# Attention of the first eight pairs in four 64x64 tiles of the array, two pairs at a time, with another order of the early work

## The chip, the core and the metric

The kernel runs on one core of a Trainium2 chip. The metric is the device time of one launch in microseconds, as the median of several runs. Before the change it is 834.56 us (three runs, 834.26 to 834.79). PE is the matrix engine, PEld its loading of stationary operands; DVE, ACT and POOL are the vector, scalar and general engines; SP issues nearly all DMAs.

## The reference

Attention over blocks of 64 positions, for 8 batches of 576 positions and 8 heads of 64, and then a feed-forward layer with g = h - tanh(h):

```python
q_c = q.reshape(B, H, nc, chunk, D)            # chunk = D = 64; k_c, v_c alike
scores = scale * np.matmul(q_c, k_c.transpose(0, 1, 2, 4, 3))
scores = scores - np.max(scores, axis=-1, keepdims=True)
attn = np.exp(scores)
attn = attn / (np.sum(attn, axis=-1, keepdims=True) + 1e-09)
out = np.matmul(attn, v_c)
...
x = np.ascontiguousarray(attn_out.transpose(0, 2, 1, 3)).reshape(B * S, H * D)   # 4608 x 512
h = x @ w_in          # 512 x 2048
g = h - np.tanh(h)
return (g @ w_out).astype(np.float32)
```

The weights arrive as 64-bit floats, 16.8 MB, and are made into 32-bit ones in the kernel.

## The kernel before, in words

The 4608 tokens are 36 **pairs**: 128 tokens, two blocks of 64 positions, all 8 heads. Four pairs are a **group** of the feed-forward layer, nine groups in all. Groups 2 to 8 have another attention (class `Late`, f16) and another feed-forward; the change leaves them alone. It is about the **early pairs** 0 to 7, the tokens of groups 0 and 1, and about the order of the work up to the end of group 0.

An early pair p goes through these steps (class `Early`; the letter is its token in the plan):

- `a`, `v`: DMAs of q and k, and of v. q and v lie in tiles `qbd`, `vbd` twice as wide, whose other half is zero, so that the product of a 128-row operand gives two blocks at a time on the whole array. The zeros are written once, at the start, by DVE and ACT (L172, L174).
- `S`: scores, 8 f32 products of 128x128 by 128x64 into a PSUM bank (L195).
- `M` or `E`: the maximum of each row (DVE, L202), then either subtraction on DVE and one exponent on ACT (`M`), or eight exponents on ACT that also sum (`E`, L213).
- `N` or `n`: sums, reciprocals and division of the weights, on DVE (`N`, L228) or by head on ACT (`n`, L226).
- `T`: four transposes on PE (L156), copied from PSUM by ACT (`aT`).
- `V`: values, 8 products (L243), and the result as a rounded part `xh` (ACT, L250) and a rest `xl` (DVE, L251).

The weights of the feed-forward come in 16 units `fc`. `l` loads a half of a unit (part 0 of w_in, part 1 of w_out; three buffers), `c` converts: one ACT and three DVE instructions put the bits together (L141 to L144), then ACT rounds to `wh` and DVE takes the rest `wl` (L148, L149). `g` is gemm1 of a unit (12 products `xh wh`, `xh wl`, `xl wh`, L552) with h - tanh(h) behind it (ACT L563, DVE L564) and a split into `gh` and `gl` (ACT L571, DVE L572). `h` is gemm2 of the oldest unit that is split (12 products, L581). With a part behind the dot, `l`, `c` and `g` do a half; half a gemm1 covers two pairs. `F` is a number of idle products on a tile of zeros, which nothing reads (L819).

The text `PLAN` (L55) is the order of these tokens. Left of the bar, SP and PE run in just the order written, while the order on the other engines follows a scheduler; right of it the place in the text is a rank, and a scheduler lays out all engines. `Y` ends the first pair of PSUM banks, after which scores, transposes and values have one pool of two banks; `Z` frees the attention's tiles for the later weights. In every case each engine's order is fixed when the program is built, and an instruction that waits holds up all behind it on its engine.

## Time and profile before

| | before |
|---|---|
| median of 3 runs | 834.56 us |
| the profiled execution's own time | 834.37 us |
| its span | 832.5 us |
| PE busy | 819.0 us, 98% of the span |
| DVE, ACT, POOL busy | 650.1, 474.6, 375.0 us |
| DMA | 63.17 MB, 234 GB/s in the first fortieth of the span |
| first gemm1 of group 0 | 27.70 us |
| last gemm2 of group 0 | ends about 142.4 us |

A busy PE is not a PE at its peak: the ends of products are modelled and overlap, so a row's duration is longer than the distance to the next. In a row of the timeline, the first number is the start, the second the length in us, then engine, line, operation, what is written and read, shape and count. A group of instructions by line shows busy time in us, then the mean of one in ns, then the engine's idle time before them.

### The profile page before, as it was taken

What the parts mean: (1) busy time and instruction counts of PE and PEld (TensorE: products, weight loads), DVE (VectorE), ACT (ScalarE), POOL (GpSimd) and SP (SyncE); (2) the same over time, 40 slices, a digit from 0 to 9 for tenths busy, and PEclk for the clock granted to TensorE, in tenths of its full rate; (3) what the DMA queues carried; (4) which work ended last, traced back from release to release, by engine and by line L of the source; (5) the groups of instructions that cost most, each with busy time, mean ns of one, the idle gap of its engine ahead of it and who ended that gap; (6) DMA issues with size and microseconds to landing.
All of it is one profiled execution on the core that took longest, in us unless ns stands there. A gap on an engine that the chain in (4) does not pass through costs nothing.

```text
span 832.5 us, 20121 instructions
## 1 busy us (share of the span) xinstructions
PE 819.0 (98%) x8546; PEld 686.5 (82%) x8546; DVE 650.1 (78%) x879; ACT 474.6 (57%) x779; POOL 375.0 (45%) x380
## 2 busy tenths in 40 slices
PE   8999999999999999999999999999999999999997
PEld 6888777778866657878888888888888888888886
DVE  5897797785755998899787878787878787877553
ACT  6798785865453546674565456545654564454332
POOL 0000000000015874857575757575757575757563
PEclk9999999999999999999999999999999999999999
DMA  9865245131110212322222322222222220302000
GB/s 234 238 223 165 103 153 172 55 102 53 27 52 1 78 26 78 77 78 52 78 52 77 53 78 51 78 51 78 52 78 51 78 52 3 52 2 51 2 27 26
DMA packets 64858, 63.17 MB, mean 76 GB/s; under 512 B 33024, under 2 KB 47360, under 8 KB 64768
## 3 DMA queue, kind: packets, MB, share of 16 engines
q1 hardware_dynamic: 64480, 61.62, 26.5%
q8 instruction: 67, 1.10, 0.6%
q10 hardware_dynamic: 288, 0.26, 0.1%
q14 instruction: 23, 0.19, 0.1%
HBM read 45.09 MB, written 9.44 MB: 65 GB/s over the span
## 4 chain that ended last, share of the span: by engine, by line
PE 85%; DVE 8%; POOL 2%; issue 2%; ACT 1%; DMA 1%; SPq 0%; DVEq 0%; ACTq 0%
PE ph L649 28%; PE po L689 25%; PE po L581 13%; PE ph L552 12%; PE psa L343 3%; PE psa L195 2%; PE psa L243 1%; DVE gl L572 1%; DVE w L143 1%; DMA vbd<-vE 1%; DVE w L144 1%; DVE wh L515 1%; DMA k<-kE 0%; DVE wl L515 0%; DVE wl L149 0%
## 5 line engine op out<-in xcount | busy, mean ns | idle before, releaser
L649 PE MATMUL ph<-xh,wl 128*128 128x256 f16 x2160 | 249.6, 273 | 0.0
L649 PEld LDWEIGHTS <-wl 128*128 128x128 f16 x2160 | 209.9, 98 | 25.1 <-issue 0.5
L658 POOL TENSOR_TENSOR xl<-xl 128x256 f32<-128x256 f32 x96 | 96.9, 1009 | 184.1 <-DVE xl L657 183.4
L656 ACT ACTIVATE t<-ph,sig 128x512 f32<-128x512 f32 x96 | 65.8, 685 | 147.8 <-PE ph L649 147.1
L689 PEld LDWEIGHTS <-wh 128*128 128x128 f16 x1008 | 98.6, 98 | 11.4
L657 DVE SCALAR_TENSOR_TENSOR xl<-ph,sig,t 128x512 f32<-128x512 f32 x96 | 71.6, 746 | 46.6 <-ACT t L656 46.4
L659 POOL TENSOR_TENSOR xl<-xl 128x128 f32<-128x128 f32 x96 | 105.4, 1098 | 0.0
L660 POOL TENSOR_TENSOR xl<-xl 128x256 f32<-128x256 f32 x96 | 92.9, 968 | 0.0
L689 PE MATMUL po<-wl,wh 128*128 128x256 f16 x576 | 89.7, 273 | 0.0
L670 DVE SCALAR_TENSOR_TENSOR wh<-xl,to_g,wh 128x896 f16<-128x896 f32 x48 | 64.6, 1346 | 30.0 <-ACT wh L669 30.0
L669 ACT ACTIVATE wh<-xl,to_g 128x896 f16<-128x896 f32 x48 | 49.9, 1039 | 60.7 <-POOL xl L660 60.7
L581 PE MATMUL po<-wh,gh 128*128 128x512 f32 x192 | 79.1, 412 | 0.7 <-ACT gh L571 0.7
L670 DVE SCALAR_TENSOR_TENSOR gl<-xl,to_g,gh 128x896 f16<-128x896 f32 x48 | 71.9, 1498 | 8.9 <-ACT gh L669 8.7
L552 PE MATMUL ph<-xh,wl 128*128 128x512 f16 (+2 forms) x324 | 77.1, 375 | 0.0
L581 PE MATMUL po<-wh,gl 128*128 128x512 f32 x192 | 75.3, 397 | 1.0 <-DVE gl L572 1.0
L689 PE MATMUL po<-wh,wh 128*128 128x256 f16 x432 | 75.9, 273 | 0.0
L581 PE MATMUL po<-wl,gh 128*128 128x512 f32 x192 | 75.5, 393 | 0.0
L689 PEld LDWEIGHTS <-gh 128*128 128x128 f16 x672 | 64.9, 98 | 7.8
L458 POOL PARTITION_ALL_REDUCE whole<-sums x1 | 0.4, 445 | 131.9 <-DMA rawv<-vL 131.9
L689 PE MATMUL po<-wh,gh 128*128 128x256 f16 x336 | 54.4, 273 | 0.0
L572 DVE TENSOR_TENSOR gl<-t,gh 128x512 fp32r<-128x512 f32 (+1 forms) x52 | 40.2, 776 | 17.9 <-ACT gh L571 15.6
L689 PE MATMUL po<-wl,gh 128*128 128x256 f16 x336 | 52.4, 273 | 0.0
(158 smaller groups left out, 1502.6 us busy)
## 6 DMA issues: line engine op xcount, KB each, us to landing
raw<-w_in SPq DMA_DIRECT2D x16, 512.0 KB, 3.8
raw<-w_out SPq DMA_DIRECT2D x16, 512.0 KB, 5.6
rawk<-kL SPq DMA_DIRECT2D x28, 256.0 KB, 3.5
rawv<-vL SPq DMA_DIRECT2D x28, 256.0 KB, 3.5
xl<-qL SPq DMA_DIRECT2D x28, 256.0 KB, 2.9
out<-wh SPq DMA_DIRECT2D x46, 128.0 KB, 1.8
qbd<-qE SPq DMA_DIRECT2D x16, 128.0 KB, 4.2
k<-kE SPq DMA_DIRECT2D x8, 256.0 KB, 4.8
```

The costliest lines, as they stand in the source:

```text
L552: nc.tensor.matmul(ph, lhsT=self.weight(fc, 0, a)[:, kc * P:(kc + 1) * P], rhs=x[b][:, kc, cols], start=(k == 0), stop=(k == 3 * KC - 1))
L572: nc.vector.tensor_sub(gl, t, gh)
L581: nc.tensor.matmul(self.po[t], lhsT=gg[a][:, ts], rhs=self.weight(fc, 1, b), start=(fc == 0 and i == 0), stop=(fc == FC - 1 and i == 2))
L649: nc.tensor.matmul(self.ph[:, 1 - f::2, :], lhsT=half_w[fc][:, w, kc * P:(kc + 1) * P], rhs=rhs, start=(k == 0), stop=(k == 3 * KC - 1))
L656: nc.scalar.activation(t, self.ph, AF.Tanh, scale=sig)
L657: nc.vector.scalar_tensor_tensor(out=u[:, :4], in0=self.ph, scalar=sig, in1=t, op0=ALU.mult, op1=ALU.subtract)
L658: nc.gpsimd.tensor_add(u[:, 4:6], u[:, 1:3], u[:, 0:4:3])
L659: nc.gpsimd.tensor_add(u[:, 6], u[:, 1], u[:, 2])
L660: nc.gpsimd.tensor_sub(u[:, 0:4:3], u[:, 0:2], u[:, 2:4])
L669: nc.scalar.activation(gh, u, AF.Copy, scale=powers[1])
L670: nc.vector.scalar_tensor_tensor(out=gl, in0=u, scalar=powers[1], in1=gh, op0=ALU.mult, op1=ALU.subtract)
L689: nc.tensor.matmul(place[m], lhsT=part[:, self.SUM[m]], rhs=w[m][:, o], start=first, stop=(last and part is gl), skip_group_check=True)
```

## The change

q, k and v of the early pairs are laid out anew, and `p` in the tokens `a`, `S`, `v` now stands for one block (of 64 positions) of both pairs of a couple: rows 0 to 63 of its tile belong to the first pair, rows 64 to 127 to the second. There are no zeros. Each product has a 64x64 stationary operand in one of the four quarters of the array; a method `products` gives them out, quarter after quarter. Two PSUM banks take a couple's scores, one bank per pair, and each bank is filled half by the first `S` and half by the second. The values of both pairs are computed at the second of them, and their result is written by two copies and two subtractions for two pairs. The DMAs write 2 KB per row in one piece where they wrote 512 bytes at a time. The plan is a new text. It has 21 idle products where there were 29, six `E` and two `M` where there were five and three, two `n` and six `N` where there were three and five.

```diff
 PLAN = """
-a0 a1 l0.0 l0.1 a2 v2 F4 F1 v0 F4 S0 v1 l1.0 S1 l1.1 F1 c0 F1 a3 F6 l2.0 c1 F1 E0 N0 T0 S2 F4 l3.0 M1 M2 n1 T1 N2 V0 V1 F7 v3 S3 T2 g0.0 M3 V2 l2.1 N3 T3 V3 | g1.0 c2 l3.1 a4 l4.0 l4.1 v4 g0.1 h c3.0 Y S4 l5.0 g2.0 a6 g3.0 E4 c3.1 h n4 a5 l5.1 c4.1 h l6.0 c4.0 l7.0 g2.1 h g3.1 v6 l6.1 h l7.1 c5 S5 E5 g1.1 g4 S6 E6 h N5 c7.0 n6 g7 c6.0 l8.0 v5 a7 v7 T4 h T5 l8.1 V5 c7.1 c6.1 g6 T6 V4 l9.0 h V6 S7 E7 N7 T7 V7 Z l10.0 h c8 l11.0 h l11.1 l10.1 l9.1 g5 c9 g8 g9 c10.0 h c10.1 l12.0 c11 h l13.0 l12.1 c12 g10 l14.0 h h c13.0 g11 l14.1 l15.0 h g12 l13.1 l15.1 c13.1 g13 h h c14.0 c14.1 c15 h g14 g15 h h
+l0.0 a0 a1 l0.1 F9 S0 S1 v0 v1 E0 M1 c0.0 l1.0 l1.1 a2 F8 N0 T0 a3 N1 T1 c0.1 F4 V0 c1.0 v2 v3 S2 S3 g0.0 l2.0 c1.1 E2 M3 g1.0 h l2.1 N2 T2 N3 T3 h V2 l3.0 | c2 l3.1 Y g0.1 g1.1 h a4 a5 l4.0 l4.1 S4 S5 v4 v5 c3 E4 E5 g2 h l5.0 l5.1 n4 N5 c4 g3 h T4 T5 V4 a6 a7 l6.0 l6.1 c5 g4 h S6 S7 v6 v7 c6 E6 E7 l7.0 l7.1 g5 h n6 N7 c7 T6 T7 V6 Z g6 h l8.0 l8.1 c8 g7 h l9.0 l9.1 c9 g8 h l10.0 l10.1 c10 g9 h l11.0 l11.1 c11 g10 h l12.0 l12.1 c12 g11 h l13.0 l13.1 c13 g12 h l14.0 l14.1 c14 g13 h l15.0 l15.1 c15 g14 h g15 h h
 """
...
-        def __init__(self, pool, psum, bufs, zeros):
+        def __init__(self, pool, psum, bufs):
...
-            self.qbd, self.vbd = (
-                [pool.tile([P, 4, P, 2], F32, name=f"{n}{i}", bufs=1) for i in range(bufs)] for n in ("qbd", "vbd")
-            )
...
+        def bank(self, p):
+            return self.psum[p // 2 % len(self.psum)].tile([P, 2, 4, CH], F32, name="psa")
 
         def load(self, p):
...
-            for c in range(2):
-                r = slice(c * CH, (c + 1) * CH)
-                nc.sync.dma_start(out=d["q"][r, :, r], in_=qE[p, c])
-            nc.sync.dma_start(out=d["k"], in_=kE[p])
+            for n, src in (("q", qE), ("k", kE)):
+                t = self.st[p][n] = self.pool.tile([P, H, CH], F32, name=n, bufs=self.bufs)
+                nc.sync.dma_start(out=t, in_=src[p])
...
+        def products(self, out, stationary, moving):
+            for hp in range(4):
+                for i, u in ((0, 0), (1, 1), (0, 1), (1, 0)):
+                    r = slice(i * CH, (i + 1) * CH)
+                    nc.tensor.matmul(out(i, hp)[u * D:(u + 1) * D], lhsT=stationary(r, hp, u), rhs=moving(r, hp, u), start=True, stop=True)
 
         def scores(self, p):
...
-            for h in range(H):
-                nc.tensor.matmul(ps[:, h, :], lhsT=d["q"][:, h // 2, :, h % 2], rhs=d["k"][:, h, :], start=True, stop=True)
+            if p == first:
+                for c in range(2):
+                    self.st[first + c]["sp"] = self.bank(p)
+            ps = [self.st[first + c]["sp"] for c in range(2)]
+            self.products(lambda c, hp: ps[c][:, p - first, hp], lambda r, hp, u: d["q"][r, 2 * hp + u], lambda r, hp, u: d["k"][r, 2 * hp + u])
...
         def values(self, p):
...
-            for hp in range(4):
-                for c in range(2):
-                    cs = slice(c * CH, (c + 1) * CH)
-                    nc.tensor.matmul(ps[:, hp, cs], lhsT=d["v"][:, hp, :, c], rhs=d["aT"][:, hp, cs], start=True, stop=True)
+            first = p // 2 * 2
+            ps = self.st[first]["vps"] = [self.bank(p) for _ in range(2)]
+            for c in range(2):
+                d = self.st[first + c]
+                self.products(lambda e, hp: ps[e][:, c, hp], lambda r, hp, u: d["v"][r, 2 * hp + u], lambda r, hp, u: d["aT"][r, hp, u * CH:(u + 1) * CH])
 
         def result(self, p, x, i):
...
-            nc.scalar.copy(out=xh[:, :, ts], in_=ps)
-            nc.vector.tensor_sub(xl[:, :, ts], ps, xh[:, :, ts])
+            for e, ps in enumerate(self.st.pop(p)["vps"]):
+                xh, xl = (t[:, :, ts].rearrange("p hp (c e q) -> p e c hp q", c=2, e=2)[:, e] for t in x)
+                nc.scalar.copy(out=xh, in_=ps)
+                nc.vector.tensor_sub(xl, ps, xh)
```

Line numbers behind `Early` are 7 lower in the changed kernel (L545 is L552 of before, L574 is L581).

How the order moves is shown at three places. The first is PE, from the values of the first pairs to the first gemm1. `psa<-aT,...` are values, `psa<-k,...` scores, `psa<-ident,s` transposes. Before (seven idle products stand ahead of these rows, and the values of pairs 0 and 1 ahead of those):

```order
L195 MATMUL psa<-k_218,qbd_132 128x64 x8
L156 MATMUL psa<-ident,s 128x128 x4
L552 MATMUL ph<-xh,wh_70 128x256 x4
L552 MATMUL ph<-xh,wl_71 128x256 x4
L552 MATMUL ph<-xl,wh_70 128x256 x4
L243 MATMUL psa<-aT,vbd_135 128x64 x8
```

Now:

```order
L177 MATMUL psa<-aT,v 64x64 x32
L177 MATMUL psa<-k,q 64x64 x32
L545 MATMUL ph<-xh,wh_70 128x256 x4
L545 MATMUL ph<-xh,wl_71 128x256 x4
L545 MATMUL ph<-xl,wh_70 128x256 x4
L545 MATMUL ph<-xh,wh_74 128x256 x4
```

Scores and values of two pairs stand together, and both come ahead of the first gemm1; the transposes of pairs 2 and 3 come after two half gemm1 and half a gemm2, all eight of them at once.

The second place is DVE at the same time, from the results of the first pairs on (`xl`), with the maxima `mx` of pairs 2 and 3. Before:

```order
L251 TENSOR_TENSOR xl<-psa,xh 128x4x128
L220 RECIPROCAL sm<-sm 128x8
L228 TENSOR_TENSOR s<-s,sm 128x512
L142 TENSOR_SCALAR w<-w 128x1024
L143 SCALAR_TENSOR_TENSOR w<-raw,w 128x1024
L144 SCALAR_TENSOR_TENSOR w<-raw,w 128x1024
L202 TENSOR_REDUCE mx<-psa 128x8
L208 TENSOR_TENSOR s<-psa,mx 128x512
```

Now:

```order
L244 TENSOR_TENSOR xl<-psa,xh 128x2x4x64 x2
L192 TENSOR_REDUCE mx<-psa 128x8 x2
L201 TENSOR_SCALAR mx<-mx 128x8
L142 TENSOR_SCALAR w<-w 128x1024
L198 TENSOR_TENSOR s<-psa,mx 128x2x4x64
L557 TENSOR_TENSOR t<-ph,t 128x256
L143 SCALAR_TENSOR_TENSOR w<-raw,w 128x1024
L565 TENSOR_TENSOR gl<-t,gh 128x256
```

Both maxima now stand behind the results of the first two pairs; before, pair 2 was already being divided there.

The third place is PE behind the scores of pairs 4 and 5: two gemm1 with half a gemm2 between them, and the transposes of these pairs. Before, the scores of one pair, other work, and the scores of the next:

```order
L195 MATMUL psa<-k_588,qbd_130 128x64 x8
L552 MATMUL ph<-xh,wh_74 128x256 x4
L552 MATMUL ph<-xh,wl_75 128x256 x4
L552 MATMUL ph<-xl,wh_74 128x256 x4
L552 MATMUL ph<-xh,wh_86 128x512 x4
L552 MATMUL ph<-xh,wl_87 128x512 x4
L552 MATMUL ph<-xl,wh_86 128x512 x4
L195 MATMUL psa<-k_529,qbd_131 128x64 x8
```

Now, from the second of the two gemm1 on:

```order
L545 MATMUL ph<-xh,wh_82 128x512 x4
L545 MATMUL ph<-xh,wl_83 128x512 x4
L545 MATMUL ph<-xl,wh_82 128x512 x4
L226 MATMUL psa<-ident,s 128x128 x6
L545 MATMUL ph<-xh,wh_86 128x512
```

The transposes of both pairs, six of eight at first, stand right behind that gemm1.

More of the change, by code (lines that the diff above doesn't have):

```diff
@@ new lines, in bank @@
+        def bank(self, p):
+            return self.psum[p // 2 % len(self.psum)].tile([P, 2, 4, CH], F32, name="psa")
+        def load(self, p):
+            for n, src in (("q", qE), ("k", kE)):
+                t = self.st[p][n] = self.pool.tile([P, H, CH], F32, name=n, bufs=self.bufs)
+                nc.sync.dma_start(out=t, in_=src[p])
+        def load_values(self, p):
+            v = self.st[p]["v"] = self.pool.tile([P, H, D], F32, name="v", bufs=self.bufs)
+            nc.sync.dma_start(out=v, in_=vE[p])
@@ L197, in largest @@
         def largest(self, p):
             d = self.st[p]
-            d["s"] = self.pool.tile([P, H, CH], F32, name="s", bufs=2)
-            d["mx"] = self.pool.tile([P, H, 1], F32, name="mx", bufs=2)
-            d["sm"] = self.pool.tile([P, H, 1], F32, name="sm", bufs=2)
-            nc.vector.reduce_max(out=d["mx"][:, :, 0], in_=d["sp"], axis=AX.X)
+            d["s"] = self.pool.tile([P, 4, 2, CH], F32, name="s", bufs=3)
+            d["mx"] = self.pool.tile([P, 2, 4, 1], F32, name="mx", bufs=3)
@@ L204, in exponents @@
+            d["sm"] = self.pool.tile([P, 4, 2, 1], F32, name="sm", bufs=3)
+            nc.vector.reduce_max(out=d["mx"].rearrange("p e hp k -> p (e hp k)"), in_=d["sp"].rearrange("p e hp k -> p (e hp) k"), axis=AX.X)
         def exponents(self, p, summed):
@@ L211, in exponents @@
             nc.vector.tensor_scalar_mul(d["mx"], d["mx"], -scale)
-            for h in range(H):
-                nc.scalar.activation(d["s"][:, h, :], d["sp"][:, h, :], AF.Exp, bias=d["mx"][:, h, :], scale=scale, accum_out=d["sm"][:, h, :])
+            for e in range(2):
+                for hp in range(4):
+                    nc.scalar.activation(d["s"][:, hp, e, :], d["sp"][:, e, hp, :], AF.Exp, bias=d["mx"][:, e, hp, :], scale=scale, accum_out=d["sm"][:, hp, e, :])
         def sums(self, p):
@@ L230, in transpose @@
         def transpose(self, p):
-            self.st[p]["aps"] = transposed(self.pool, self.psum[p % len(self.psum)], self.st[p]["s"])
+            d = self.st[p]
+            d["aps"] = self.bank(p).rearrange("p a b k -> p (a b k)").rearrange("p (hp n) -> p hp n", hp=4)
+            for hp in range(4):
+                nc.tensor.transpose(d["aps"][:, hp, :], d["s"][:, hp].rearrange("p e k -> p (e k)"), ident)
         def weights(self, p):
-            aT = self.st[p]["aT"] = self.pool.tile([P, 4, P], F32, name="aT", bufs=min(self.bufs, 2))
+            aT = self.st[p]["aT"] = self.pool.tile([P, 4, P], F32, name="aT", bufs=3)
@@ L235, in weights @@
             nc.scalar.copy(out=aT, in_=self.st[p]["aps"])
         def values(self, p):
-            d = self.st[p]
-            ps = d["vps"] = self.psum[p % len(self.psum)].tile([P, 4, P], F32, name="psa")
-            for hp in range(4):
-                for c in range(2):
-                    cs = slice(c * CH, (c + 1) * CH)
-                    nc.tensor.matmul(ps[:, hp, cs], lhsT=d["v"][:, hp, :, c], rhs=d["aT"][:, hp, cs], start=True, stop=True)
-        def result(self, p, x, i):
-            xh, xl = x
-            d = self.st.pop(p)
-            ps = d["vps"]
-            ts = slice(i * P, (i + 1) * P)
-            nc.scalar.copy(out=xh[:, :, ts], in_=ps)
-            nc.vector.tensor_sub(xl[:, :, ts], ps, xh[:, :, ts])
+            first = p // 2 * 2
@@ L799, in attn_ffn_kernel @@
     make_identity(nc, ident)
-    att = Early(pool, [psum, ps_a], 4, warm)
+    att = Early(pool, [psum, ps_a], 4)
     idle = ps_h.tile([P, MOST], F32, name="ph")
```

45 lines of the change are left out of this document (16 added, 29 removed).

## The prediction

> **What bounds the kernel now.** I read the page's busy shares first, then the time windows of the stage that the change touches, then the chain of waits inside it. The page and the windows (columns: stretch, its length, busy time and instruction count of PE, PEld, DVE, ACT, POOL, then the granted clock, DMA share, GB/s):
>
> ```profile
> PE 819.0 (98%) x8546; PEld 686.5 (82%) x8546; DVE 650.1 (78%) x879; ACT 474.6 (57%) x779; POOL 375.0 (45%) x380
> ...
> 16.50:27.70 11.20, 11.20 (x89) 9.96 (x88) 9.92 (x17) 8.09 (x21) 0.00 (x0) 1.00 1.07 299
> 27.70:39.00 11.30, 10.54 (x75) 9.13 (x74) 10.84 (x19) 7.86 (x18) 0.00 (x0) 1.00 0.73 194
> 39.00:60.00 21.00, 20.94 (x148) 19.23 (x147) 19.14 (x39) 19.14 (x64) 0.00 (x0) 1.00 0.68 219
> 60.00:80.00 20.00, 20.00 (x119) 17.16 (x119) 15.35 (x31) 17.60 (x59) 0.00 (x0) 1.00 0.50 156
> 80.00:100.00 20.00, 18.90 (x98) 15.33 (x98) 14.43 (x24) 13.99 (x39) 0.00 (x0) 1.00 0.42 154
> 100.00:142.40 42.40, 42.08 (x182) 33.19 (x181) 37.65 (x71) 32.98 (x71) 0.82 (x2) 1.00 0.41 134
> ```
>
> PE is the bound and has almost no holes after 16.5 us. Group 0 of the feed-forward ends at 142.4 us. Behind it PE's instructions are row for row the same in both kernels, so what group 0's end moves, the whole time moves. But DVE is no idle bystander: 10.84 of 11.30 us between 27.7 and 39.0, where the first softmaxes and the first weights compete for it. Less PE work helps only where DVE keeps up.
>
> **What the products cost.** From the chain of waits (start, us, what), then the timeline of PE asked up to 52.56, 52.67 and 52.78 us, and up to 171.10, 171.126 and 171.15 us:
>
> ```profile
> 39.17 0.88 PE psa L195 x8
> ...
> 58.74 1.82 PE psa L195 x16
> 60.56 2.85 PE po L581 x12
> 63.42 0.44 PE psa L156 x4
> ```
>
> ```profile
> 52.49 0.34 PE L195 MATMUL psa<-k,qbd 128*128 128x64 f32 x2
> 52.49 0.45 PE L195 MATMUL psa<-k,qbd 128*128 128x64 f32 x3
> 52.49 0.57 PE L195 MATMUL psa<-k,qbd 128*128 128x64 f32 x4
> ...
> 171.07 0.22 PE L343 MATMUL psa<-a,wh 64*64 64x64 f16 x4
> 171.07 0.25 PE L343 MATMUL psa<-a,wh 64*64 64x64 f16 x5
> 171.07 0.26 PE L343 MATMUL psa<-a,wh 64*64 64x64 f16 x8
> ```
>
> One pair's scores are 8 instructions and 16 records: an f32 product runs as two records on the same place of the array. 16 records take 1.82 us, 0.114 each. The first two start within 0.07 us of each other, the next 0.11 later each: the 64 columns stream in under 0.07, and the 128-column weights set the pitch. Values (L243) cost the same. So 8 pairs cost 16 x 1.82 = 29 us.
>
> In 64x64 tiles the weights have half the columns, so I estimate the pitch of one tile at half of 0.114, 0.06 us. How many tiles run together is the first unknown. The f16 rows show four records within 0.03 us, but the fifth, which needs the first tile again, starts only after 171.10, and 6 to 8 come behind it: a record whose tile is busy holds up all behind it. In f32 the second record of each product is such a record. So one product overlaps with the first record of the next alone, and costs one pitch: 32 products of two pairs take 32 x 0.06 = 1.9 us instead of 3.64. From below: four tiles always full, 64/4 x 0.06 = 0.96. From above: no overlap, 64 x 0.06 = 3.8. I take 1.9, because the f16 rows show the blocking itself. Each change between tiles and whole array I estimate at 0.1 us (the gap ahead of the first f16 tile record, 171.07, behind a product that began 0.33 before and streams 2.85/12 = 0.24), 0.2 per group.
>
> **The start.** From the timeline:
>
> ```profile
> 6.32 7.06 PE L195 MATMUL psa<-k,qbd 128*128 128x64 f32 x32 [1.12 <-DMA k<-kE]
> 13.17 3.72 PE L819 MATMUL ph<-warm 128*128 128x512 bf16 x9
> 17.16 2.00 PE L195 MATMUL psa<-k,qbd 128*128 128x64 f32 x16
> 18.99 1.03 PE L819 MATMUL ph<-warm 128*128 128x512 bf16 x4
> 20.29 3.88 PE L243 MATMUL psa<-aT,vbd 128*128 128x64 f32 x32
> ```
>
> The idle products (L819) take 0.41 us each at 13.17 and 0.26 at 18.99; scores take 0.22 a record at 6.32 and 0.12 at 17.16. PE runs at half clock until the end of the nine idle products. 7 us of scores alone did not lift it. How quickly the clock goes again, the end of the kernel shows (timeline of PE, then windows):
>
> ```profile
> 826.30 0.49 PE L689 MATMUL po<-wl,wh 128*128 128x256 f16 x3
> ...
> 826.80:828.80 2.00, 0.00 (x0) 0.00 (x0) 1.79 (x5) 0.17 (x1) 1.72 (x3) 1.00 0.01 3
> 828.80:830.80 2.00, 0.00 (x0) 0.00 (x0) 0.00 (x0) 0.00 (x0) 0.00 (x0) 0.50 0.78 262
> ```
>
> It fell to half 2 us after the last product. Now the changed start. SP loads one weight (0.52 MB) and four attention tiles (1.05 MB) before the first scores; from 2.1 us on, at 361 to 233 GB/s, that lands at 6.5 to 9 us. I take 8.5:
>
> ```profile
> 0.00:20.00 20.00, 17.71 (x76) 12.28 (x77) 11.43 (x23) 12.98 (x37) 0.69 (x6) 1.00 0.92 233
> 8.00:10.00 2.00, 2.00 (x12) 2.00 (x11) 0.00 (x0) 0.00 (x0) 0.00 (x0) 1.00 1.03 361
> ```
>
> Scores of pair 1 at half clock take 16 x 0.12 = 1.9, end 10.4 (before: 13.4). No softmax can begin sooner, since each bank now needs both halves. Then F8 keeps PE busy to 13.8. DVE's new order until s of pair 1 is divided counts 17 instructions. Their durations by form, and two single rows of the timeline:
>
> ```profile
> L149 DVE TENSOR_TENSOR wl<-w,wh 128x512 fp32r<-128x512 f32 x32 | 21.1, 686 | 2.2 <-ACT wh L148 2.1
> L144 DVE SCALAR_TENSOR_TENSOR w<-raw,w 128x1024 uint32<-128x1024 uint32 x9 | 10.9, 1215 | 0.1
> L143 DVE SCALAR_TENSOR_TENSOR w<-raw,w 128x1024 uint32<-128x1024 uint32 x9 | 10.9, 1221 | 0.1
> L142 DVE TENSOR_SCALAR w<-w 128x1024 uint32<-128x1024 uint32 x9 | 6.2, 687 | 0.0
> L142 DVE TENSOR_SCALAR w<-w 128x512 uint32<-128x512 uint32 x14 | 5.6, 417 | 0.3 <-ACT w L141 0.2
> L202 DVE TENSOR_REDUCE mx<-psa 128x8 f32<-128x512 f32 x8 | 5.5, 689 | 8.6 <-PE psa L195 8.6
> L220 DVE RECIPROCAL sm<-sm 128x8 f32<-128x8 f32 x8 | 1.6, 195 | 0.1
> ...
> 23.98 0.68 DVE L251 TENSOR_TENSOR xl<-psa,xh 128x512 fp32r<-128x512 f32 x1
> ...
> 34.40 0.69 DVE L228 TENSOR_TENSOR s<-s,sm 128x512 f32<-128x512 f32 x1
> ```
>
> Ten of 0.69 (128x512 forms, halves of L143 and L144 among them), two of 0.42, five of 0.17 to 0.2: 8.65 us. Such sums come out 6% long, since ends overlap: before, the 20 rows from 23.98 to 35.09 sum to 11.8 and took 11.1. So 8.1, and pair 1 is divided at 18.5. Between 13.8 and then PE has nothing but four transposes, 5 us, more than the 2 us in which the clock fell. So F4 (1.7), the values of pairs 0 and 1 (32 x 0.12 = 3.8) and the scores of 2 and 3 (3.8) run at half clock: 18.5 + 0.9 (transposes) + 1.7 + 3.8 + 3.8 = 28.7. From there DVE has the rows from the two maxima to the division of pair 3: 20 instructions, 11.3 us, less 6% is 10.6, plus 0.8 for the late first gemm1: 40.1. The last transposes (0.45), h of unit 1 (6 x 0.24 = 1.4) and the values of 2 and 3 (1.9) end at 43.9. Before, this same state, values of pair 3 done and the next scores about to start, is reached at 39.1 (row 39.17). **Late by 4.8 us.** What would hide it is the product work ready at that time, but PE's fixed order puts the transposes of 2 and 3 ahead of it. The new layout takes away DVE's and ACT's zeroing of the first 6 us; that time was not waited for past the first scores.
>
> **The rest of group 0.** Before: 142.4 - 39.1 = 103.3 us, of which about 99.5 is work (16 units of 24 products at 0.23 less the 5.6 done is 83, 8 x 1.82 of scores and values, 4 x 0.44 of transposes), 3.8 waiting. Now the work is less by 8 x 1.82 - 4 x 1.9 = 7.0, plus 6 x 0.2 of switching: 93.7. Waiting grows. First, behind the division of pair 3 DVE has two whole weights, 2 x (0.69 + 1.22 + 1.22) = 6.3 us, and then the result of pairs 2 and 3 (xl, 1.4): 7.7. PE has 3.75 until the values are done, waits 1.2 for two copies on ACT (0.6 each, as a 128x512 form), has 16 products of 0.12, and waits 0.9 for xl: 2.0 in all. Second, transposes 4 and 5 come 7.0 us of PE work behind their scores (two gemm1 of 2.8, half a gemm2), and their chain has these rows (timeline of ACT):
>
> ```profile
> 11.00 0.31 ACT L213 ACTIVATE s<-psa,mx 128x64 f32<-128x64 f32 x1 [3.98 <-DVE mx L211]
> ...
> 13.23 0.24 ACT L213 ACTIVATION_READ_ACCUMULATOR s<-psa,mx 128x1 f32 x1
> ...
> 17.84 2.02 ACT L226 ACTIVATE s<-s,sm 128x64 f32<-128x64 f32 x8
> ```
>
> Eight exponents take 13.47 - 11.00 = 2.5, both pairs 4.8 to 4.9; two maxima 1.4, DVE's backlog 1.1, a tanh 0.6, six divisions 1.5: 9.5, so PE waits 2.5. Third, the same at 6 and 7 with 8.2 us ahead, 1.5 to 2. With 0.8 for the rest, 7.3 us of waiting; it could be 4 or 11. So 101.0 instead of 103.3.
>
> Sum: +4.8 - 2.3 = +2.5 on the profiled execution's 834.4 us (the median shown, 834.56, is 0.2 above it): **837**. The late weights are no new bound: from 43.9 on DVE has 13 x 4.5 us of weights, 15 x 1.4 of shrinking and 9 of attention, some 88 of 101 us.
>
> **Rivals.**
>
> A, the forecast, 53%: half clock through the start, two records overlapping, 837; its own range 833 to 841.
>
> B, the clock is lifted by F8 and stays, 12%. Then 18.5 + 0.45 + 0.95 + 1.9 + 1.9 = 23.7, plus 10.6 is 34.3, and the state stands at 38.1, 1.0 ahead: 834.4 - 1.0 - 2.3 = 831. For it: 3.4 us of F after 2 us of scores. Against it: the 5 us hole and the fall at 828.8. [...]
>
> C, faster, four f32 tiles at once, 15%. The scores end 0.95 sooner, values and scores at half clock 1.9 each, the values of 2 and 3 0.95: the state comes at 38.2, and of the later 4 x 0.95 about half is not eaten by the waits: 834.4 - 0.9 - 2.3 - 2 = 829. For it are the four f16 records within 0.03 us, against it the fifth. [...]
>
> D, the change doesn't do what it says, 7%: f32 records in tiles don't overlap at all. 3.8 instead of 1.9 per group, twice that at half clock, gives 1.9 + 3.8 + 3.8 + 1.9 + 4 x 1.9 = 19 more: 856. Against it is the f16 overlap.
>
> E, 13%: the waits of the rest stay at before's 3.8, since DVE's late work finds gaps: 837 - 3.5 = 833.5.
>
> **How the numbers follow.** A run of this kernel tells 0.2%, 1.7 us, from no change. A is slower by more than that in two thirds of its 53, D always, E and B rarely: 47%. C nearly always, B mostly, half of E and an eighth of A are faster: 34%. The rest, 19%, is no change. The likeliest case gives 837. The range 829 to 842.5 holds A, B, E and half of C, and leaves out D.
>
> **What would show it.** In the profile after: scores of two pairs in 1.9 us at full clock (0.96 is C, 3.8 is D); the first gemm1 (L545) near 28.7 (B: 23.7) with the granted clock at half before it; the values of pair 3 done near 44; PE holes ahead of the transposes L226 of pairs 4 to 7, released by ACT or DVE s; group 0's last gemm2 near 145. I am wrong if the clock is full at 20 us, or if DVE's chains turn out shorter than their summed rows.

## The result, and the profile after

| | before | after |
|---|---|---|
| median, same chip | 834.67 us (4 runs, 834.26 to 835.12) | 826.96 us (4 runs, 825.69 to 829.37) |
| ratio | | 0.9911, 95% interval 0.9888 to 0.9934 |
| profiled execution, its span | 834.37, 832.5 us | 826.73, 825.0 us |
| PE, DVE, ACT busy | 819.0, 650.1, 474.6 us | 801.1, 645.2, 469.8 us |
| first gemm1 | 27.70 us | 23.38 us |
| values of pair 3 done | 39.1 us | 37.83 us |
| last gemm2 of group 0 starts | 142.13 us | 133.31 us |

The change is 7.7 us faster, 0.9%; 837 and "late" were forecast. Group 0 ends 8.8 us sooner, and of that 1.2 are lost again later. First the page's busy shares of the profile after:

```profile
PE 801.1 (97%) x8770; PEld 664.4 (81%) x8770; DVE 645.2 (78%) x852; ACT 469.8 (57%) x769; POOL 375.1 (45%) x380
```

Then its windows (same columns as before). Up to the first change of clock on record, at 20.3 us here and 16.4 us in the kernel before, the windows print 1.00 whatever the clock was; there the durations of the rows tell it.

```profile
16.50:27.70 11.20, 9.27 (x164) 7.12 (x164) 9.99 (x18) 8.75 (x29) 0.00 (x0) 1.00 1.03 398
27.70:39.00 11.30, 6.22 (x83) 4.40 (x81) 10.89 (x18) 7.86 (x18) 0.00 (x0) 0.85 0.55 199
39.00:60.00 21.00, 19.48 (x153) 15.54 (x153) 18.37 (x34) 19.54 (x68) 0.00 (x0) 1.00 0.63 226
60.00:80.00 20.00, 18.95 (x252) 14.80 (x253) 14.84 (x26) 19.38 (x68) 0.00 (x0) 1.00 0.31 106
80.00:100.00 20.00, 20.00 (x109) 16.32 (x102) 19.48 (x27) 18.05 (x35) 0.00 (x0) 1.00 0.38 134
100.00:133.50 33.50, 33.50 (x148) 27.51 (x147) 28.48 (x51) 21.73 (x45) 0.83 (x2) 1.00 0.40 141
```

PE, full before from 16.5 us on, now has holes up to 80 us: 11.30 - 6.22 = 5.1 between 27.7 and 39, of which 3.9 are for DVE's divisions (DVE is busy 10.89 of 11.30) and 1.2 for a copy on ACT, 1.5 and 1.05 in the two rows behind. The change took away PE work, and part of it came back as waiting. Now the timeline of PE (in brackets, the idle time before the row and what ended it):

```profile
6.10 1.13 PE L177 MATMUL psa<-k,q 64*64 64x64 f32 x32 [0.91 <-DMA k<-kE]
7.94 1.13 PE L177 MATMUL psa<-k,q 64*64 64x64 f32 x32 [0.71 <-DMA k<-kE]
9.01 3.60 PE L812 MATMUL ph<-warm 128*128 128x512 bf16 x8
...
16.85 1.09 PE L226 MATMUL psa<-ident,s 128*128 128x128 f32 x4 [0.19 <-DVE s L220]
17.73 1.91 PE L812 MATMUL ph<-warm 128*128 128x512 bf16 x4
19.57 1.46 PE L177 MATMUL psa<-aT,v 64*64 64x64 f32 x64
20.86 1.10 PE L177 MATMUL psa<-k,q 64*64 64x64 f32 x62
23.18 0.27 PE L177 MATMUL psa<-k,q 64*64 64x64 f32 x2 [1.21 <-issue]
23.38 0.74 PE L545 MATMUL ph<-xh,wh 128*128 128x256 f32 x4
...
33.21 0.63 PE L226 MATMUL psa<-ident,s 128*128 128x128 f32 x4 [1.65 <-DVE s L220]
...
36.13 1.70 PE L177 MATMUL psa<-aT,v 64*64 64x64 f32 x64
39.01 0.73 PE L545 MATMUL ph<-xh,wh 128*128 128x256 f32 x4 [1.18 <-ACT xh L243]
...
54.17 1.03 PE L226 MATMUL psa<-ident,s 128*128 128x128 f32 x6 [1.07 <-ACT s L218]
...
60.30 1.18 PE L177 MATMUL psa<-aT,v 64*64 64x64 f32 x64
...
75.66 1.04 PE L226 MATMUL psa<-ident,s 128*128 128x128 f32 x6 [1.05 <-ACT s L218]
```

Four things are to be seen. The values of two pairs (64 records) take 1.18 us at 60.30; without the 0.22 of the last record that is 0.96 for 63 starts, 0.0152 each. The idle products take 3.60 for eight at 9.01, 0.45 each against the 0.26 at 18.99 in the kernel before, so half clock, and 64 values take 1.70 at 36.13, half clock again (0.50 on record from 33.94 to 37.35). The last two records of the scores wait 1.21 for "issue", nothing that the profile shows. And the holes ahead of the transposes of pairs 4 to 7 are there, 1.07 and 1.05.

### The profile page after: what moved, and what is told of

It is laid out like the page before. It is cut to its first block, busy times and chain, and to the rows that moved or that the text cites. A ratio compares the mean times of both kernels' runs of the same rounds, so it can differ in the third digit from the quotient of the medians.

```text
span 825.0 us, 20504 instructions
## 1 busy us (share of the span) xinstructions
PE 801.1 (97%) x8770; PEld 664.4 (81%) x8770; DVE 645.2 (78%) x852; ACT 469.8 (57%) x769; POOL 375.1 (45%) x380
## 4 chain that ended last, share of the span: by engine, by line
PE 84%; DVE 8%; ACT 4%; POOL 2%; issue 1%; DMA 1%; SPq 0%; DVEq 0%; ACTq 0%
PE ph L642 28%; PE po L682 26%; PE po L574 13%; PE ph L545 12%; PE psa L336 3%; ACT s L204 2%; DVE gl L565 1%; PE psa L177 1%; DMA k<-kE 1%; DVE wh L508 1%; DVE wl L508 0%; DVE gl L663 0%; DVE mx L192 0%; DVE w L143 0%; DVE wh L326 0%
## 5 line engine op out<-in xcount | busy, mean ns | idle before, releaser
L651 POOL TENSOR_TENSOR xl<-xl 128x256 f32<-128x256 f32 x96 | 94.2, 981 | 185.7 <-DVE xl L650 185.5
L652 POOL TENSOR_TENSOR xl<-xl 128x128 f32<-128x128 f32 x96 | 108.2, 1127 | 0.0
L653 POOL TENSOR_TENSOR xl<-xl 128x256 f32<-128x256 f32 x96 | 93.1, 970 | 0.0
L574 PE MATMUL po<-wh,gh 128*128 128x512 f32 x192 | 79.0, 411 | 1.0 <-ACT gh L564 1.0
L574 PE MATMUL po<-wh,gl 128*128 128x512 f32 x192 | 75.8, 396 | 1.0 <-DVE gl L565 1.0
L545 PE MATMUL ph<-xh,wl 128*128 128x512 f16 (+2 forms) x316 | 76.3, 379 | 0.0
L574 PE MATMUL po<-wl,gh 128*128 128x512 f32 x192 | 75.7, 394 | 0.0
```

What stands on the lines that cost most here:

```text
L545: nc.tensor.matmul(ph, lhsT=self.weight(fc, 0, a)[:, kc * P:(kc + 1) * P], rhs=x[b][:, kc, cols], start=(k == 0), stop=(k == 3 * KC - 1))
L574: nc.tensor.matmul(self.po[t], lhsT=gg[a][:, ts], rhs=self.weight(fc, 1, b), start=(fc == 0 and i == 0), stop=(fc == FC - 1 and i == 2))
L651: nc.gpsimd.tensor_add(u[:, 4:6], u[:, 1:3], u[:, 0:4:3])
L652: nc.gpsimd.tensor_add(u[:, 6], u[:, 1], u[:, 2])
L653: nc.gpsimd.tensor_sub(u[:, 0:4:3], u[:, 0:2], u[:, 2:4])
```

## The experiments

My theory after the result was: four f32 tiles run together (rival C of the forecast), the start came sooner through it and through faster transfers, and DVE and ACT set the rest. The order of the runs follows that. "End" is the start of the last gemm2 of group 0 in the profile, 133.31 in the change. It scatters less than the time, since what comes behind is the same work in every kernel. But each end is that of one profiled execution, and in a second profile of the unaltered change (the control, further down) it is 132.76, so differences up to 0.6 us are not told by it.

### How many tiles at once

```diff
-            for hp in range(4):
-                for i, u in ((0, 0), (1, 1), (0, 1), (1, 0)):
+            for i, u in ((0, 0), (1, 1), (0, 1), (1, 0)):      # one tile; for two: pairs of quarters,
+                for hp in range(4):                            # all hp of the first pair, then of the second
```

> The changed kernel with its products in another order: two of the four tiles take all their products, then the other two, so that at most two different tiles ever stand next to each other. Theory (records of different tiles run together, records of one tile follow each other at one pitch of 0.058 us): 64 records of two pairs take 1.86 us at full clock instead of 0.93, 3.4 instead of 1.7 at half. On the path of the start +0.9 (scores of 1), +0.9 (values 0 and 1), +0.9 (scores 2 and 3), +1.7 (values 2 and 3 in the half-clock window), behind that 4 x 0.93 with a part hidden in waits, about 2.8: in all +7, 834 us (831 to 836). This is the world that the forecast took for the likeliest, so what is left to its 837 is the error of its other steps. Rival (the four records that start together are both passes of two products, not four tiles): 0.93 us still, 827 us.

> The same with all products of one tile before the next tile's. Theory: no two different tiles next to each other but at three borders, so 64 records take 3.7 us at full clock; three times the extra of two tiles, +18 to +22: 845 to 849 us. Rival (both passes of two products at once): 1.86 us, 831 to 836 us.

Measured: two tiles 827.15 us (ratio to before 0.9924, 0.9899 to 0.995), end 134.11; one tile 832.30 (0.998, 0.997 to 0.999), end 139.36. The timeline of PE at full clock, two tiles, with one record that stands alone:

```profile
20.93 0.22 PE L177 MATMUL psa<-k,q 64*64 64x64 f32 x1
...
60.71 1.73 PE L177 MATMUL psa<-aT,v 64*64 64x64 f32 x64
```

and one tile:

```profile
62.56 1.70 PE L177 MATMUL psa<-aT,v 64*64 64x64 f32 x38
```

Less the 0.22 of the last record: (1.73 - 0.22) / 63 = 0.024 us a record with two tiles, (1.70 - 0.22) / 37 = 0.040 with one, 0.0152 with four. So the records of different tiles do run together, and the rival is out. But one tile alone is faster than I and the expectation had it (0.040, not 0.058), so four tiles gain 2.6 times, not four times.

The time was the surprise. Two tiles cost 1.6 times as much PE time per product and the kernel is as fast. Only at 2.6 times as much does it lose 5 us. Up to about 1.5 us per 64 records the products are not what sets the time; between 1.5 and 2.5 nothing was measured. Where the saved work went is seen from the end of the values of pair 3 to the end of group 0, two tiles and then one tile:

```profile
38.29:134.50 96.21, 93.98 (x645) 76.16 (x646) 82.33 (x135) 79.78 (x215) 0.82 (x2) 1.00 0.42 148
```

```profile
42.22:139.75 97.53, 96.65 (x646) 79.98 (x646) 83.14 (x135) 79.74 (x215) 0.83 (x2) 1.00 0.41 146
```

With one tile PE works 96.65 and waits 0.9, with two 93.98 and 2.2, with four 92.03 and 3.7 (the window is shown further down). The order of the products is all that differs: of 4.6 us of work saved, 2.9 came back as waits.

### The plan alone

The kernel before with the text of the new plan (each `V` followed by that of its partner, three buffers for the softmax tiles); array, zeros and transfers as before.

```diff
-a0 a1 l0.0 l0.1 a2 v2 F4 F1 v0 F4 S0 v1 l1.0 S1 ...
+l0.0 a0 a1 l0.1 F9 S0 S1 v0 v1 E0 M1 c0.0 l1.0 l1.1 a2 F8 N0 T0 a3 N1 T1 c0.1 F4 V0 V1 ...
```

> The kernel before (128x128 array with zeros, its own transfers and zeroing) under the changed plan, with the scores, softmax and waits of two pairs in a row as the plan has them; three buffers for the softmax tiles as in the change. It tells the plan's own share. Theory that the tiles carry the gain: the products cost 3.64 us per two pairs as one tile at a time does, the transfers are the slow ones, so 846 to 853 us, the plan alone being 12 to 18 us slower than the kernel before. Rival (the plan carries the gain, tiles are a side show): 830 us or less.

Measured: 838.06 us, ratio 1.0072 (1.0041 to 1.0102). Three of ten executions took 844 to 847, the others 836 to 838; the profiled one is of the long kind, and its timeline and windows show where the clock was:

```profile
21.92 6.93 PE L243 MATMUL psa<-aT,vbd 128*128 128x64 f32 x32
28.64 7.03 PE L195 MATMUL psa<-k,qbd 128*128 128x64 f32 x32
```

```profile
27.70:39.00 11.30, 11.30 (x58) 11.30 (x58) 4.32 (x8) 3.91 (x16) 0.00 (x0) 0.54 1.05 255
```

PE is busy without a hole, with f32 products of the whole array, and the clock is 0.54 in that stretch: values and scores of two pairs take 14 us. The clock is half from about 21 to 38 us (0.65 granted from 16.5 to 27.7 us, 0.54 from 27.7 to 39), though PE has no hole from 20.10 on, and full only behind the start of the first gemm1 (35.43): its last four products before 38 us take 0.98, the next four, at 38.10, 0.64. So 17 us of a PE that is busy by the record did not lift the clock here; why was not tested. The long executions have a mean granted clock of 0.980 to 0.989, the others 0.992 to 0.998, which fits, though none of the others was profiled. The new plan alone is about 4 us slower than the kernel before; under it the new array is worth about 838.06 - 826.96 = 11 us (measured on two chips). Of these 5.8 come with 64x64 operands, wide rows and no zeroing even when only one tile runs (832.30), 5.2 with the second tile, and none with four.

### Wide and narrow rows

The same transfers, with q, k and v stored so that a row is 512 bytes:

```diff
-                nc.sync.dma_start(out=t, in_=src[p])
+                nc.sync.dma_start(out=t.rearrange("p (a h) k -> p a (h k)", a=4), in_=src[p].rearrange("a p n -> p a n"))
```

> The changed kernel with q, k and v of the first eight pairs stored so that a row of a transfer is 512 bytes as before, not 2 KB; number of transfers and bytes are unchanged. Theory (the short rows, not the number of transfers, held the rate to 230 to 300 GB/s of the start): the rate to 20 us falls from 390 to under 300 GB/s, q and k of pair 1 land at 8.5 to 9 instead of 7.8, those of pair 3 at 21 to 22 instead of 15.7, +1 to +3 us: 828 to 830. Rival (the rate was held down by issue costs or by the zeroing): rate and time as in the change, 827.

Measured: 827.21 us (0.9918, 0.9903 to 0.9932), end 134.17. Windows of this kernel:

```profile
8.00:16.50 8.50, 4.66 (x40) 2.02 (x40) 6.09 (x14) 5.55 (x24) 0.00 (x0) 0.64 1.11 338
16.50:27.70 11.20, 8.84 (x164) 6.79 (x164) 10.43 (x20) 8.19 (x25) 0.00 (x0) 0.85 1.10 351
```

351 GB/s stand against 398 with wide rows. The short rows cost 12% of the rate, not the whole way down to the 299 of the kernel before in the same window; what the rest of that is (its q and v went to 64 partitions at a time) was not tried. The scores of 1 start at 9.11 instead of 7.94, near the 8.5 to 9 expected, and group 0 ends 0.86 later; but a kernel with wide rows has them at 9.00 too (pairs 4 and 6, below), so not all of that need be the rows. The rate under 300 and the 1 to 3 us of time that the theory expected did not come.

### The clock

Idle products in the holes, and the same kernel without the 8 and the 4 behind the first scores:

```diff
-... a2 F8 N0 T0 a3 N1 T1 c0.1 F4 V0 ... g1.0 h l2.1 N2 T2 N3 T3 ...
+... a2 F20 N0 T0 a3 N1 T1 c0.1 F4 V0 ... g1.0 h F10 l2.1 N2 T2 F7 N3 T3 ...
+... a2 N0 T0 a3 N1 T1 c0.1 V0 ... g1.0 h l2.1 N2 T2 N3 T3 ...
```

> The changed kernel with 20 idle products instead of 8 ahead of the first transposes, and 10 and 7 more in the holes ahead of the transposes of pairs 2 and 3. Theory (the granted clock at 16.9 to 20.3 and 33.9 to 37.4 us sits on the path): the clock is full from about 13 to 16 us on and stays so, the transposes, four idle products and the first values take 1.5 less, the last of gemm2 and the values of 2 and 3 1.7 less: 823.5 to 825.5 us. Rival (DVE, busy 10.9 of 11.3 us there, sets the time of these steps): the half-clock stretch vanishes and the time stays, 826 to 827.5. Third: the hole of 1.2 us ahead of the last product of the scores of 3, if it hangs on the number of PE instructions before it, comes 12 instructions earlier in PE's order.

> The changed kernel without the 8 and the 4 idle products behind the first scores. Theory (idle products buy the clock): transposes, values of 0 and 1, scores of 2 and 3 and the first gemm1 run at half clock, 0.9 + 0.9 + 2.8 more, less the 1.8 of the four idle products: first gemm2 1 to 3 us later, 828 to 830 us. Rival (it is hidden): 826 to 827.5. The hole ahead of the last product of the scores of 3: if it hangs on the number of PE instructions it comes 12 later, within the first gemm1; if it hangs on these products it stays where it is.

Measured: held 825.33 us (0.990, 0.9876 to 0.9923), end 132.99; without 827.16 (0.9913, 0.9897 to 0.993), end 134.23. The windows of the change, cut to the grid on which its clock changes (at 20.29, 33.94, 37.35, 358.21 and 361.62 us, whole multiples of 3.41 apart), and then of the held one:

```profile
27.11:30.53 3.42, 1.56 (x6) 0.87 (x6) 2.94 (x7) 3.42 (x12) 0.00 (x0) 1.00 0.39 119
30.53:33.94 3.41, 1.36 (x10) 1.14 (x11) 3.19 (x9) 3.39 (x8) 0.00 (x0) 1.00 0.88 342
33.94:37.35 3.41, 3.41 (x50) 2.47 (x52) 3.41 (x4) 0.52 (x1) 0.00 (x0) 0.50 0.70 254
...
354.80:358.21 3.41, 1.47 (x101) 1.12 (x99) 3.41 (x3) 3.07 (x5) 3.41 (x3) 1.00 0.31 79
358.21:361.62 3.41, 3.41 (x17) 2.37 (x18) 3.41 (x5) 2.05 (x3) 1.46 (x2) 0.50 0.71 231
```

```profile
33.94:37.35 3.41, 3.07 (x74) 2.38 (x74) 3.19 (x4) 1.46 (x3) 0.00 (x0) 1.00 0.86 320
```

A window of 3.41 us in which PE was busy for 1.36 or 1.47 us is followed by one at half clock; one with 1.56 is not, and of the windows of the kernel before at full clock the least busy that kept it has 2.01 (364.58 to 367.99). So few windows do not show a border. The second such place, 358 us, is a wait in the attention of a later group and can cost half of 3.41 us, an estimate from the length of the window and its clock of 0.50. What follows group 0 (the profiled time less the start of the last gemm2) takes 693.2 to 693.8 us in eleven of the seventeen profiles, 693.4 in the change, and 691.7 to 692.2 in the other six, 692.2 in the kernel before. From group 0's end to the last products the change has the half clock in this window alone, and the kernel before has it nowhere. Two more of the six (two tiles, weight last) run on at full clock behind the same wait, four products of gemm2 in 0.61 where the change takes 0.99. By this I take the window for the 1.2 us that are lost.

Holding the clock through 33.9 to 37.4 us was meant to save 1.7 us there, and group 0 ends 0.3 sooner. The 20 idle products did not hold it ahead of that: at 17.11 four transposes take 1.09 in that kernel, against 0.63 at 15.84, and at 17.99 four idle products 1.91: half clock there too. Taking away the idle products costs 0.9 at the end, and nothing in the time that can be told; 825.33 for the held one lies in the theory's range, but its interval holds the rival's too.

Two stretches have to be told apart. Up to the transposes of pair 3 (33.89 held, 33.36 without, 33.21 in the change) the clock is not on the path: DVE is (27.7 to 39: 10.89 of 11.30). From there to the end of the values of 3 it is: 3.1 us with the clock full, 4.6 in the change with one window at half, 5.4 without idle products, at half clock from the transposes (1.09 for four) to the values (1.86 for 64). Of the 1.5 that the held one wins there, it loses 0.7 ahead of it (0.3 of that by scores that landed later) and 0.5 in the rest of group 0; the kernel without carries 0.9 of its 1.0 to the end of group 0.

The clock of the start is also not the same in every execution. In the two profiles of "weight last" (below), the same kernel, the second scores take 1.13 us at 7.84 in one and 0.69 at 7.59 in the other, and the idle products behind them 5.34 and 4.49 for twenty.

The two runs also settle the hole of 1.2 us. With 12 more idle products it stands 12 records earlier, with 12 fewer 12 records later, then not among the scores but in the first gemm1. Timelines of PE, held and without:

```profile
23.34 0.45 PE L177 MATMUL psa<-k,q 64*64 64x64 f32 x14 [1.31 <-issue]
```

```profile
23.11 0.39 PE L545 MATMUL ph<-xl,wh 128*128 128x256 f32 x2
24.82 0.40 PE L545 MATMUL ph<-xl,wh 128*128 128x256 f32 x2 [1.31 <-issue]
```

It hangs on the number of PE's instructions, not on what they do. Twelve profiles with 64x64 tiles two or four at a time show it, each behind PE's 219th record (three of them count 218, and some records can be missing).

### The softmax on DVE or ACT

```diff
-... E0 M1 ... E2 M3 ...          second kernel:  -... E4 E5 ... E6 E7 ...
+... M0 M1 ... M2 M3 ...                          +... M4 E5 ... M6 E7 ...
```

> The changed kernel with the exponents of pairs 0 and 2 made in one piece (subtraction and sum on DVE) instead of eight instructions on ACT; sums and subtractions cost DVE 1.3 us more per pair, ACT 2.2 less. Theory (the softmax of the first couple, not the products, sets the start): pair 1 is divided at 15 instead of 16.6, first gemm1 1.5 sooner, 825 to 826 us. Rival (DVE is full between 27.7 and 39, so its extra 1.3 us for pair 2 takes the gain away): transposes of 3 no sooner than 33, 827 to 828.5.

> The same exchange for pairs 4 and 6 alone, where ACT is busy 19.5 of 21 and 19.4 of 20 us. Theory (what waits are left behind 39 us, 3.7 us in all, come from ACT's eight exponents ahead of the transposes of 4 to 7): the holes of 1.1 and 0.4 us there close, group 0 ends 1 to 1.5 sooner, 825.5 to 826 us. Rival (the waits come from DVE's backlog): unchanged or up to 1 us longer.

Measured: 827.10 us (0.9915, 0.9893 to 0.9937), end 132.89 (its last four gemm2 run from 132.18 to 133.29); 826.34 (0.991, 0.9891 to 0.9929), end 134.48. In the first, the transposes of pair 1 come at 16.12, 0.7 sooner where 1.6 were expected, the first gemm1 at 22.32, 1.1 sooner, the transposes of pair 3 at 32.39, 0.8 sooner, and of that 0.4 are left at the end of group 0. Against the control (16.41, 22.80, 32.64, end 132.76) it leads by 0.5 at most and ends no sooner, so even these small leads are not clear of the scatter of one kernel. In the second the first scores of pair 1 happened to land 1.1 us later (9.00 instead of 7.94), and its values of 3 are done at 39.46. From there to the end of group 0 it takes 0.5 less than the change: the hole ahead of the transposes of 4 and 5 closed, as expected, and the one ahead of 6 and 7 grew from 1.05 to 1.30. Neither moves the time by what can be told.

### Where the second half of weight 1 stands in DVE's order

Four versions of one edit, with 20 idle products instead of 8 and the exponents of pair 0 on DVE in all of them:

```diff
-... S2 S3 g0.0 l2.0 c1.1 E2 M3 g1.0 h l2.1 N2 T2 N3 T3 h V2 l3.0 | ... n4 ... n6 ...
+... S2 S3 g0.0 l2.0 E2 M3 g1.0 h F4 l2.1 N2 T2 F4 N3 T3 V2 c1.1 h l3.0 | ... n4 ... n6 ...        values first
+... as before it ...                                                   | ... N4 ... N6 ...        values first, dve
+... S2 S3 g0.0 l2.0 c1.1 E2 M3 g1.0 h F10 l2.1 N2 T2 F7 N3 T3 h V2 l3.0 | ... N4 ... N6 ...       held, dve
+... S2 S3 g0.0 l2.0 E2 M3 g1.0 h F10 l2.1 N2 T2 F7 N3 T3 c1.1 h V2 l3.0 | ... n4 ... n6 ...       weight last
```

> The changed kernel with three edits of order: 20 idle products instead of 8, the exponents of pair 0 in one piece on DVE, and the second half of weight 1 (3.1 us of DVE) moved from ahead of the softmax of pairs 2 and 3 to behind the values of 2 and 3, the gemm2 of unit 1 with it (four idle products in each hole). Theory (DVE's order ahead of the transposes sets the time of the state 'values of pair 3 done', and what comes sooner there stays sooner): that state at 33 to 35 us instead of 37.8, group 0's end 2 to 3 us sooner, 823.5 to 825. Rival (ACT, 19.5 of 21 and 19.4 of 20 us busy between 39 and 80, and DVE eat the lead): the state is sooner and group 0 ends within 0.5 us of 133.6, 825.5 to 827.

> The same, and the division of pairs 4 and 6 in one instruction on DVE (0.6 us) instead of eight on ACT (2 us each). If ACT between 39 and 80 us eats the lead, this gives it back: group 0's end 1 to 1.5 us sooner than without, 823 to 825. If DVE does, it costs up to 0.5.

> The changed kernel with the clock held by idle products (20, 10 and 7), the exponents of pair 0 in one piece and the division of pairs 4 and 6 on DVE, the order of weight 1 as in the change. If ACT between 39 and 80 is what eats leads, group 0 ends 1 to 2 us sooner than the 133.3 of its last gemm2 in the change: 824 to 825.5.

> As the first of these three with the second half of weight 1 behind the transposes of 3, but its gemm2 still ahead of the values. Theory: the transposes come 2 to 3 us sooner as there, but PE then waits 3.1 us on this weight before the values of 2 and 3, so the state is no sooner than in the change: 826 to 828.

Measured, in this order: 828.26 us (0.9932, 0.9917 to 0.9947), end 132.97; 825.57 (0.990, 0.9885 to 0.9914), end 134.22; 826.24 (0.9897, 0.9874 to 0.9919), end 133.72; 825.90 (0.9904, 0.9881 to 0.9927), end 132.16.

Most of these expectations failed. Values first brought the values of 3 to 35.6 us, but not the transposes (33.13 instead of 33.21), and its later order opened a hole of 1.45 us behind group 0, with half clock behind it, 1.96 for four products that take 1.10 at 136.47. The timeline of PE of that kernel:

```profile
139.88 1.96 PE L545 MATMUL ph<-xh,wh 128*128 128x512 f32 x4 [1.45 <-DVE t L557]
```

Taking 4 us from ACT between 39 and 80 did not bring the end forward (134.22, 133.72). Their starts differ in the clock (the first four products of gemm1 take 0.74, 1.03 and 1.22 in the first three), so the stretch from the values of 3 to the end of group 0 compares better: 97.74 with the division on DVE against 97.78 without in "values first", 96.62 against 96.37 in the "held" pair. By this ACT alone is not what eats the leads. The version from which I expected nothing had the earliest end.

### The forecast's world, and the best order against a control

The third kernel puts three terms back at once: one tile at a time, rows of 512 bytes, no idle products behind the first scores. The last two are the change itself and "weight last" once more, with more rounds, on one chip.

> The changed kernel with three terms put back at once towards what the forecast assumed: one tile's products after the other's (2.5 us per 64 records at full clock, 3.9 at half, the forecast had 1.9 and 3.8), rows of 512 bytes, and no idle products behind the first scores so that the clock comes late. Theory (the forecast's error lies in these terms, and they add): +5.3 for the tiles, +0.9 for the rows, +0.9 for the clock as group 0's end had them singly, 834 us, and more if the clock stays at half through the values and scores (up to 837). Rival (the terms hide one another, and the forecast's waits were wrong on their own): 832 to 833, no more than one tile at a time alone.

> The changed kernel itself, unaltered, as the control for the next run: 825.5 to 829 with a median near 827.

> The version of the earlier run that ended group 0 1.1 us sooner (20 idle products, exponents of pair 0 on DVE, second half of weight 1 behind the transposes of 3, idle products in the holes). Theory (the sooner end of group 0 comes through): 1 us under the control, 825.5 to 826. Rival (scatter): within 0.5 us of the control.

Measured: all back 831.79 us (0.9982, 0.9972 to 0.9992), no more than one tile at a time alone, as the rival has it. By the profiles the terms hide one another only in part at the end of group 0: it is 140.34, 1.0 later than with one tile alone, where the two other terms had 1.8 singly. The timeline of PE, and the window from the end of the values of 3 to the end of group 0:

```profile
40.19 3.53 PE L177 MATMUL psa<-aT,v 64*64 64x64 f32 x64
```

```profile
43.72:140.74 97.02, 96.15 (x645) 79.97 (x646) 82.34 (x134) 79.14 (x214) 0.83 (x2) 1.00 0.40 138
```

The values of pair 3 end at 40.19 + 3.53 = 43.72. The forecast had 43.9. That they agree is in part luck: the first gemm1 comes at 26.62 where the forecast had 28.7, the transposes of 3 at 36.61 instead of 40.1, and then the last gemm2 and the values take 7.1 instead of 3.8, mostly at half clock and with one tile at a time. So this kernel has the state of the forecast's start by other steps, and it is 0.2% faster than the kernel before all the same.

The control: 827.36 us (0.9924, 0.991 to 0.9938), end 132.76. Weight last: 824.73 (0.9897, 0.9883 to 0.991), end 131.71, ahead of the control by 1.05 in group 0 and 2.6 in the median. Its lead was 1.1 against the change's first profile, where the intervals overlapped widely; here they just touch. Of the 1.05, 0.35 are the first scores of pair 1, which happened to land sooner (7.59 instead of 7.94). The rest of the 2.6 is not in the order of group 0: both profiled executions take 693.3 us or 693.4 behind it, while the control's three longest have a granted clock of 0.984 to 0.986, and this kernel's all 0.995 to 0.998. Which of the edits gives the lead was not taken apart. It is the fastest version measured, about 1% under the kernel before and 0.1 to 0.3% under the change.

## Why the prediction was wrong, point by point

By stretch, the miss of 10 us (837 against 826.96) is 6.1 in the start, 5.2 in the rest of group 0, and 1.2 the other way behind group 0, where the forecast had no change.

**The bound** was read rightly: what moves the end of group 0 moves the time (8.8 us there, 7.7 in the time), and DVE limits 27.7 to 39 us.

**The product term**, "one product costs one pitch", 1.9 us for 32 products of two pairs: 0.97 measured. Rival C's mechanism was the right one. Both halves of the step failed. The pitch of a lone tile is 0.040, not half of 0.114; that the columns of the weights set it was an estimate, which no run took apart. And the fifth f16 record, which I took to hold up all behind it, is only the first of the next four: in f32 too the records come by four. Timeline of PE after, asked up to 60.40 and 60.43 us:

```profile
60.30 0.30 PE L177 MATMUL psa<-aT,v 64*64 64x64 f32 x4
60.30 0.33 PE L177 MATMUL psa<-aT,v 64*64 64x64 f32 x6
```

Records of one tile are 0.040 apart, so four within 0.03 us are four tiles. That the second record of a product comes behind the other tiles' first ones follows, but was only argued. Still, this term alone does not make the forecast's 837: with 1.5 us per 64 records the time is as in the change, and with 2.5, more than the forecast's 1.9, it is 832.3.

**The start**, 43.9 for "values of pair 3 done": 37.83. The scores of 1 ended at 9.07 instead of 10.4: they could begin at 7.94, within the 6.5 to 9 of which I took 8.5, and took 1.13 at half clock instead of 1.9. Pair 1 was divided at 16.7 instead of 18.5; the 17 DVE rows took 7.6 us, against 8.1, so that sum was near. From there to the first gemm1 6.7 us instead of 10.2: values and scores 2.5 instead of 7.6, since the clock was full from 20.3 us on and the tiles ran together, and the hole of 1.2 came on top, which no step had. From the maxima of pairs 2 and 3 to the division of 3, DVE's 20 instructions ran 10.1 us, forecast 10.6; the timeline of DVE after, first and last row:

```profile
22.92 1.28 DVE L192 TENSOR_REDUCE mx<-psa 128x8 f32<-128x512 f32 x2
...
32.38 0.68 DVE L220 TENSOR_TENSOR s<-s,sm 128x512 f32<-128x512 f32 x1
```

They began ahead of the first gemm1, so my 0.8 on top was not due. Behind them the last gemm2 and the values took 1.0 more than forecast, at half clock. The step "half clock through the start" held to 20.3 us in this execution, and failed for the values and scores that it was meant for; the prediction named a full clock at 20 us as what would prove it wrong.

**The rest of group 0** is the step that fails whatever the start. I had 103.3 us before, of them 99.5 work and 3.8 waits, and 101.0 now, of them 93.7 work and 7.3 waits. The windows of the same stretch, before and after:

```profile
39.17:142.40 103.23, 101.74 (x541) 84.76 (x541) 86.57 (x163) 83.54 (x231) 0.82 (x2) 1.00 0.49 160
```

```profile
37.83:133.60 95.77, 92.03 (x645) 74.22 (x646) 82.43 (x136) 79.93 (x215) 0.83 (x2) 1.00 0.42 149
```

Before, the waits were 1.5; now they are 3.7. So I had split the stretch before wrongly already (work 101.7, not 99.5), and as a change, work fell by 9.7, not 5.8, and waits grew by 2.2, not 3.5. In the kernel with the state of the forecast's start the waits are 97.02 - 96.15 = 0.9, where I had 7.3. Its work of 96.15 fits: 93.7 plus 4 times the 0.6 that its products cost over 1.9. So the waits I added up hole by hole (2.5, 1.5 to 2, 2.0, 0.8) are the error of this stretch. A product that takes longer gives DVE and ACT time to catch up and closes the hole ahead of the next transposes (0.9, 2.2 and 3.7 us of waits with one, two and four tiles); I charged long waits and slow products together. With one tile the values of 3 also come 4.4 us later, time in which DVE and ACT may have got ahead; where they come 0.9 or 1.0 later with fast products (rows of 512 bytes, no idle products) the waits are 3.7 as in the change, but a delay of 4 us with fast products was not tried. With 0.9 in place of 7.3 and 2.4 more for its products, the forecast's own sum is 837 - 6.4 + 2.4 = 833.0, and the kernel that builds its state takes 831.8.

With the forecast's own 1.9 us per 64 records nothing was run. An estimate between the kernels with 1.5 and 2.5 gives 39.9 for the values of 3 (forecast 43.9) and 96.7 for the rest (forecast 101.0). By it the other steps of the start (the landing, the clock, DVE's overlap with the first gemm1) and the waits of the rest were wrong by some 4 us each, beside the product.

**The holes** themselves were placed rightly: ahead of the transposes of 4 and 5 (1.07 measured, 2.5 forecast) and 6 and 7 (1.05, 1.5 to 2), released by ACT's division. **Rival E** had the waits stay at 3.8, and 3.7 is what they are, but by luck: they did not stay, they grew from 1.5. C's own number, 829 with the state at 38.2, is nearest to 826.96 and 37.83, in part by luck too: C had half clock through the first values and scores, and neither the hole of 1.2 nor the sooner landing.

## What to carry to other kernels

When work is taken from the busiest engine, forecast its work and its waits with one schedule, not as two sums: slack that a longer product buys is the same slack that a hole would cost. Before charging a clock state, see whether the work in it is still on the path; here the clock ahead of the transposes of 3 moved nothing that shows, the clock behind them 0.3 to 0.9 us of group 0's end, and tiles 1.6 times as slow nothing that the time tells. And do not price a tile from the whole array: a 64x64 f32 record cost 0.040 us alone against 0.114, so that even one tile at a time, with twice the records, took 2.5 us where the array with zeros took 3.64.
